# Transposing the attention weights by DMA instead of by TensorE, from the tenth group on

## The chip, the cores and the metric

The kernel runs on one core of a Trainium2 chip. A core has a matrix engine (TensorE, PE in the profile; its weight loads are shown apart as PEld), a vector engine (VectorE, DVE), a scalar engine (ScalarE, ACT), GpSimd (POOL) and SyncE (SP), each with its own instruction queue that is worked off in order, and 16 DMA engines that all queues of transfers share. The engines meet only at semaphores. The metric is the device time of one execution in microseconds. Before the change it was 306.21 us (median of three runs, 305.25 to 306.86).

## The reference

Two parts run one after the other. The first is attention within chunks of 64 tokens: q, k and v are 8 batches x 8 heads x 576 tokens x 64, and each chunk attends only to itself. The second is a two-layer network on the 4608 tokens of 512 channels that the first part gives.

```python
scores = scale * np.matmul(q_c, k_c.transpose(0, 1, 2, 4, 3))
scores = scores - np.max(scores, axis=-1, keepdims=True)
attn = np.exp(scores)
attn = attn / (np.sum(attn, axis=-1, keepdims=True) + 1e-09)
out = np.matmul(attn, v_c)
...
h = x @ w_in            # 4608x512 @ 512x2048
g = np.maximum(0.01 * h, h)
return (g @ w_out).astype(np.float32)   # @ 2048x512
```

## The kernel before

The tokens are cut into 36 groups of 128 (G, L54): two chunks for all eight heads. The network takes them in blocks of 128, 256 and 512 tokens (BLOCKS, L57). Everything is kept in SBUF as fp16; the sums are fp32 in PSUM.

**A group's attention** is a chain of stages, each a function with one letter:

- Loads and layout: groups 0 to 8 are loaded by L80 and transposed by TensorE (stage_t, L235); from group 9 on (UD, L53) whole batches are loaded by L98 from POOL's queue in pieces of 32 channels, and VectorE's block transposes bring them in place (stage_dq L273, stage_dk L281). v is loaded by L111.
- stage_s (L286): eight matmuls give the scores, tile Sp (L291).
- stage_m (L296): VectorE takes the maximum (mx, L299) and subtracts it (sh, L301).
- stage_x (L305): ScalarE takes the exponential (ex, L307).
- stage_n (L309): VectorE sums (z, L312), inverts (L314, L316) and multiplies: en (L318), the normalised weights, 128 queries x (8 heads and chunks x 64 keys), fp16.
- stage_e (L322): TensorE transposes en in four 128x128 pieces into a PSUM tile, tpe (L326).
- stage_c (L329): VectorE copies tpe to SBUF as et (L332).
- stage_v (L335): eight matmuls with the block-diagonal v tile VB as weights and et as the moving side give xp (L341), the attention's output, transposed.
- stage_a (L352): ScalarE copies xp into xT (L354), the network's input, and raises the count of tokens that the network may use.

tpe and xp share one PSUM buffer (tag "ox").

**The network** is cut into chunks of work, which `fill(n)` (L211) takes from a list in order, as far as the tokens are there. A first-layer chunk (mm1, L161) makes a 128x512 tile hT (L171) and ScalarE's leaky ReLU of it, gT (L178). A second-layer chunk (mm2, L182) is four of the sixteen matmuls into oP (L187); after the fourth, ScalarE copies oP to osb (L196) and SP issues the store to memory (L198). One chunk of the large blocks holds four matmuls with a moving side of 512 columns.

**The order** is written out by hand: there is no scheduler, so the order of the calls is the order on each engine. Groups 0 to 5 are in a list of letters (FRONT, L395). From then on one turn of the loop at L408 holds three groups at three stages, with network chunks between them:

```python
stage_s(it - 1); stage_m(it - 1)     # scores, maximum of one group
fill(2); stage_x(it - 1)
stage_e(it - 2); stage_c(it - 2)     # transpose of the group before
...                                  # layout of group it on VectorE
stage_n(it - 1)                      # en of the group of the scores
fill(2)
stage_v(it - 2); stage_a(it - 2)
fill(3 if dve else 2)
```

So en of a group is made late in one turn, is transposed in the first half of the next turn and used by stage_v in the middle of that turn. After the loop, L436 works off what is left of the network. SP's queue carries the first load of q (L138) and the 36 stores of osb, nothing else.

Of the kernel before, what the change touches and what calls it, by code (L numbers as in the profile page):

```python
# [8 lines left out]
FP16 = mybir.dt.float16  # L9
# [7 lines left out]
def kernel(  # L17
# [21 lines left out]
    nc = tc.nc  # L39
# [5 lines left out]
    CH = 64  # L45
# [5 lines left out]
    NVB = 2  # L51
    NIN = 9
    UD = 9  # L53
    G = 2 * CH  # L54

    NU = n_tok // G
    BLOCKS = [128] * 8 + [256] * 4 + [512] * 5  # L57

    sbp = ctx.enter_context(tc.tile_pool(name="k_sb", bufs=1))
# [11 lines left out]
    def load_qk(u):  # L71

        both = []
        for name, src in (("q_in", q), ("k_in", k)):
            t = sbp.tile([128, H, D], FP16, name=name, tag=name, bufs=NIN)
            r0, r1 = u * G, (u + 1) * G
            cut = min(-(-r0 // S) * S, r1) if r0 % S else r1
# [58 lines left out]
    for eng, name, src in ((nc.sync, "q_f", q), (nc.scalar, "k_f", k)):  # L136
        t = sbp.tile([128, H, D], FP32, name=name)
        eng.dma_start(out=t, in_=src[0, :, 0:G, :].rearrange("h p d -> p h d"))  # L138
        first.append(t)
# [21 lines left out]
    def mm1(j, a):  # L161
        tb, r0 = BLOCKS[j], START[j]
        nf = 512 // tb
        if j not in gT:
            tag, bufs, pad = ("gS", 6, 128) if tb == 128 else ("gT", 2, 512)
            gT[j] = sbp.tile([128, NFC, tb], FP16, name="gT", tag=tag, bufs=bufs, padded_shape=[128, NFC, pad])
        hT = psp.tile([128, nf, tb], FP32, name="hT", tag="mm", bufs=4)
        for i in range(nf):
            fc = nf * a + i
            for t in range(NT):  # L170
                nc.tensor.matmul(  # L171
                    out=hT[:, i, :],
                    lhsT=w_inT[:, t, fc * 128:(fc + 1) * 128],
                    rhs=xT[:, t, r0:r0 + tb],
                    start=(t == 0),
                    stop=(t == NT - 1),
                )
        nc.scalar.activation(  # L178
            out=gT[j][:, nf * a:nf * a + nf, :], in_=hT, func=AFT.Prelu, bias=0.0, scale=1.0, alpha=0.01
        )  # L180

    def mm2(j, ti, part):  # L182
        if part == 0:
            oP[j, ti] = psp.tile([128, d_model], FP32, name="oP", tag="mm", bufs=4)
        o = oP[j, ti]
        for fc in range(part * 4, part * 4 + 4):
            nc.tensor.matmul(  # L187
                out=o,
                lhsT=gT[j][:, fc, ti * 128:(ti + 1) * 128],
                rhs=w_outT[:, fc, :],  # L190
                start=(fc == 0),
                stop=(fc == NFC - 1),
            )
        if part == NFC // 4 - 1:
            osb = sbp.tile([128, d_model], FP32, name="osb", tag="osb", bufs=3)
            nc.scalar.activation(out=osb, in_=o, func=AFT.Copy, bias=0.0, scale=1.0)  # L196
            r0 = START[j] + ti * 128
            nc.sync.dma_start(out=out[r0:r0 + 128, :], in_=osb)  # L198
# [12 lines left out]
    def fill(n):  # L211
        for _ in range(n):
            if not chunks:
                return
            kind, j, a, p = chunks[0]
            if START[j] + BLOCKS[j] > state["tokens"]:
                return
            chunks.pop(0)
            if kind == "mm1":
                mm1(j, a)  # L220
            else:
                mm2(j, a, p)
# [12 lines left out]
    def stage_t(u):  # L235
        qt, kt = qk.pop(u)
        qp = psp.tile([128, 4, 2, CH], FP16, name="qp", tag="qp", bufs=1)
        kp = psp.tile([128, 4, 2, CH], FP16, name="kp", tag="kp", bufs=1)
        for i in range(4):
            nc.tensor.transpose(out=qp[:, i, :, :], in_=qt[:, 2 * i:2 * i + 2, :], identity=ident)  # L240
        for i in range(4):
            nc.tensor.transpose(out=kp[:, i, :, :], in_=kt[:, 2 * i:2 * i + 2, :], identity=ident)  # L242
        QP[u], KP[u] = qp, kp
# [21 lines left out]
    def cuts(u):  # L265
        r0, r1 = u * G, (u + 1) * G
        cut = min(-(-r0 // S) * S, r1) if r0 % S else r1
        return [(a // S, a % S, (a - r0) // CH, (z - a) // CH) for a, z in ((r0, cut), (cut, r1)) if a < z]

    def stage_dq(u, s):  # L270
        qz = QZ[u % NQZ]
        for b, at, e0, n in cuts(u):
            nc.vector.transpose(  # L273
                out=qz[s * CH:(s + 1) * CH, :, e0:e0 + n, s, :],
                in_=qkd[b][0][s * CH:(s + 1) * CH, :, at:at + n * CH].rearrange("p h (e t) -> p h e t", e=n),
            )

    def stage_dk(u):
        KT[u] = sbp.tile([128, 4, 2, CH], FP16, name="KT", tag="KT", bufs=3)
        for b, at, e0, n in cuts(u):  # L280
            nc.vector.transpose(  # L281
                out=KT[u][:, :, e0:e0 + n, :],
                in_=qkd[b][1][:, :, at:at + n * CH].rearrange("p h (e t) -> p h e t", e=n),
            )

    def stage_s(u):  # L286
        qz, kt = QZ[u % NQZ], KT.pop(u)
        Sp = psp.tile([128, 8, CH], FP32, name="Sp", tag="Sp", bufs=1)
        for i in range(8):
            g, e, m = i // 4, i // 2 % 2, i % 2  # L290
            nc.tensor.matmul(  # L291
                out=Sp[:, i, :], lhsT=qz[:, 2 * m + g, e, :, :], rhs=kt[:, 2 * m + g, e, :], start=True, stop=True
            )
        SP[u] = Sp

    def stage_m(u):  # L296
        Sp = SP.pop(u)
        mx = sbp.tile([128, 8], FP32, name="mx", tag="mx", bufs=2)
        nc.vector.tensor_reduce(out=mx, in_=Sp, axis=AXL.X, op=ALU.max)  # L299
        SH[u] = sbp.tile([128, 8, CH], FP32, name="sh", tag="sh", bufs=2)  # L300
        nc.vector.tensor_tensor(  # L301
            out=SH[u], in0=Sp, in1=mx.unsqueeze(2).to_broadcast((128, 8, CH)), op=ALU.subtract
        )

    def stage_x(u):  # L305
        E[u] = sbp.tile([128, 8, CH], FP16, name="ex", tag="ex", bufs=2)
        nc.scalar.activation(out=E[u], in_=SH.pop(u), func=AFT.Exp, bias=0.0, scale=SCL)  # L307

    def stage_n(u):  # L309
        ex = E.pop(u)  # L310
        z = sbp.tile([128, 8], FP32, name="z", tag="z", bufs=2)
        nc.vector.tensor_reduce(out=z, in_=ex, axis=AXL.X, op=ALU.add)  # L312
        ze = sbp.tile([128, 8], FP32, name="ze", tag="ze", bufs=2)
        nc.vector.tensor_scalar_add(out=ze, in0=z, scalar1=1e-9)  # L314
        zi = sbp.tile([128, 8], FP32, name="zi", tag="zi", bufs=2)
        nc.vector.reciprocal(out=zi, in_=ze)  # L316
        E[u] = sbp.tile([128, 8, CH], FP16, name="en", tag="en", bufs=2)
        nc.vector.tensor_tensor(  # L318
            out=E[u], in0=ex, in1=zi.unsqueeze(2).to_broadcast((128, 8, CH)), op=ALU.mult
        )  # L320

    def stage_e(u):  # L322
        en = E.pop(u)
        tpe = psp.tile([128, 4, 128], FP16, name="tpe", tag="ox", bufs=1)
        for i in range(4):
            nc.tensor.transpose(out=tpe[:, i, :], in_=en[:, 2 * i:2 * i + 2, :], identity=ident)  # L326
        TP[u] = tpe

    def stage_c(u):  # L329
        tpe = TP.pop(u)  # L330
        et = sbp.tile([128, 2, 2, 2, CH], FP16, name="et", tag="et", bufs=2)
        nc.vector.tensor_copy(out=et, in_=tpe)  # L332
        ET[u] = et

    def stage_v(u):  # L335
        et = ET.pop(u)
        xp = psp.tile([128, NT, 2, CH], FP32, name="xp", tag="ox", bufs=1)
        for e in range(2):
            b, c = divmod(2 * u + e, NCH)
            for t in range(NT):  # L340
                nc.tensor.matmul(  # L341
                    out=xp[:, t, e, :],
                    lhsT=VB[b % NVB][:, t, c, :],
                    rhs=et[:, t // 2, e, t % 2, :] if u < UD else et[:, t % 2, e, t // 2, :],
                    start=True,
# [6 lines left out]
    def stage_a(u):  # L352
        xp = XP.pop(u)
        nc.scalar.activation(out=xT[:, :, u * G:(u + 1) * G], in_=xp, func=AFT.Copy, bias=0.0, scale=1.0)  # L354
        state["tokens"] = (u + 1) * G

# [51 lines left out]
    for it in range(6, NU + 2):  # L408
        dve = UD <= it < NU
        if it <= NU:  # L410
            stage_s(it - 1)
            stage_m(it - 1)
        if dve:
            stage_dq(it, 0)
        fill(2)
        if it <= NU:
            stage_x(it - 1)
        stage_e(it - 2)
        stage_c(it - 2)
        if dve:  # L420
            stage_dq(it, 1)
            stage_dk(it)
        elif it < UD:
            stage_t(it)
            stage_q(it)
            stage_k(it)
        if it <= NU:
            stage_n(it - 1)
        fill(2)
        stage_v(it - 2)  # L430
        stage_a(it - 2)
        fill(3 if dve else 2)
        for b in range(3, B):
            if it == 9 * b // 2 - 4:
                load_qk_batch(b)
# [31 lines left out]
```

## Time and profile before

| | |
|---|---|
| Median of the runs | 306.21 us |
| The profiled execution | 305.16 us, of which 303.4 us is the span from first to last instruction |
| PE matmul, busy | 291.9 us, 2616 instructions |
| VectorE, busy | 194.5 us, 368 instructions |
| ScalarE, busy | 155.6 us, 267 instructions |
| Granted TensorE clock | 0.999 |
| DMA moved | 28.45 MB, 177500 packets |
| tpe matmuls (L326) | 144, 219 ns each |
| et copies (L332) | 36, 417 ns each |

The duration of a matmul in this table is from its start to the modelled end of its result. Matmuls overlap one another, so what one costs in TensorE's queue is the distance from its start to the next one's start, not this duration. The page's list of groups gives busy time, mean duration, and the idle time of the engine just before the group with what ended it; the timeline gives starts and lengths in order; the list of DMA issues gives the time from issue to landing.

### The profile page before, as it was taken

How to read it: one execution, taken by the hardware profiler on the slowest of the kernel's cores; microseconds unless marked ns; L12 is line 12 of the kernel's file. 1: busy time of each engine (PE TensorE's matmuls, PEld its weight loads, DVE VectorE, ACT ScalarE, POOL GpSimd, SP SyncE). 2: the span in 40 equal slices, each digit the busy share in tenths (PEclk: the TensorE clock that was granted, in tenths of full speed). 3: DMA queues.
4: the chain of work that ended last, by engine and by line, in shares of the span. 5: the costliest groups of instructions: out<-in, count | busy, mean ns of one | idle time of the engine just before them, and what ended most of it. 6: DMA issues, size and time to landing. Idle time of an engine off the chain costs nothing.

```text
span 303.4 us, 6278 instructions
## 1 busy us (share of the span) xinstructions
PE 291.9 (96%) x2616; PEld 181.8 (60%) x2616; DVE 194.5 (64%) x368; ACT 155.6 (51%) x267; POOL 119.6 (39%) x148
## 2 busy tenths in 40 slices
PE   5879999999999999999999999999999999999994
PEld 5878965777777676868555555555555554444441
DVE  3766876778888888788888887888888840000000
ACT  5346753555556473636377337723773377226411
POOL 8557656999008832970088329700000000000000
PEclk9999999999999999999999999999999999999999
DMA  9999999999909992999099939991101110011011
GB/s 129 167 192 166 197 161 177 166 139 159 131 37 59 127 120 41 127 110 100 35 91 95 115 82 123 80 97 69 37 0 37 69 37 0 35 70 36 0 69 70
DMA packets 177500, 28.45 MB, mean 94 GB/s; under 512 B 168768, under 2 KB 172864, under 8 KB 177472
## 3 DMA queue, kind: packets, MB, share of 16 engines
q0 software_dynamic: 170208, 18.10, 105.9%
q1 hardware_dynamic: 6224, 9.70, 9.0%
q8 instruction: 20, 0.33, 0.4%
q10 hardware_dynamic: 1040, 0.26, 0.4%
q14 instruction: 8, 0.07, 0.1%
HBM read 36.70 MB, written 9.44 MB: 152 GB/s over the span
## 4 chain that ended last, share of the span: by engine, by line
PE 83%; DMA 10%; POOL 4%; issue 1%; ACT 0%; ACTq 0%; POOLq 0%
PE oP L187 39%; PE hT L171 37%; DMA w_inT<-in_moe_w_in_dram 6%; DMA VB<-in_v_dram 5%; PE xp L341 2%; PE Sp L291 2%; PE tpe L326 2%; POOL VB L111 1%; POOL k_in L80 1%; POOL q_in L80 1%; POOL w_outT L130 1%; POOL w_inT L118 0%; ACT osb L196 0%; PE kp L242 0%; PE qp L240 0%
## 5 line engine op out<-in xcount | busy, mean ns | idle before, releaser
L171 PE MATMUL hT<-xT,w_inT 128*128 128x128 f16 (+2 forms) x1088 | 135.7, 279 | 1.8 <-DMA w_inT<-in_moe_w_in_dram 1.8
L187 PE MATMUL oP<-w_outT,gT 128*128 128x512 f16 x576 | 133.8, 379 | 0.1
L171 PEld LDWEIGHTS <-w_inT 128*128 128x128 f16 x1088 | 83.3, 98 | 37.4 <-issue 1.9
L178 ACT ACTIVATE gT<-hT 128x512 f16<-128x512 f32 x144 | 85.7, 597 | 37.5 <-PE hT L171 37.2
L187 PEld LDWEIGHTS <-gT 128*128 128x128 f16 x576 | 53.3, 98 | 55.3 <-issue 0.2
L98 POOL DMA_DIRECT2D q_d<-in_q_dram x48 | 38.8, 821 | 57.1 <-DVE QZ L273 53.3
L196 ACT ACTIVATE osb<-oP 128x512 f32<-128x512 f32 x36 | 21.5, 597 | 72.8 <-PE oP L187 69.9
L299 DVE TENSOR_REDUCE mx<-Sp 128x8 f32<-128x512 f32 x36 | 24.9, 691 | 33.2 <-PE Sp L291 33.1
L98 POOL DMA_DIRECT2D k_d<-in_k_dram x48 | 38.6, 815 | 0.4
L273 DVE STREAM_TRANSPOSE QZ<-q_d 64x512 f16<-64x512 f16 (+1 forms) x60 | 38.2, 644 | 0.8
L354 ACT ACTIVATE xT<-xp 128x512 f16<-128x512 f32 x36 | 21.4, 594 | 18.7 <-PE xp L341 18.7
L307 ACT ACTIVATE ex<-sh 128x512 f16<-128x512 f32 x36 | 22.5, 625 | 9.4 <-DVE sh L301 9.2
L312 DVE TENSOR_REDUCE z<-ex 128x8 f32<-128x512 f16 x36 | 23.5, 653 | 3.5 <-ACT ex L307 3.4
L318 DVE TENSOR_TENSOR en<-ex,zi 128x512 f16<-128x512 f16 x36 | 24.9, 692 | 1.2
L301 DVE TENSOR_TENSOR sh<-Sp,mx 128x512 f32<-128x512 f32 x36 | 24.9, 691 | 1.2
L111 POOL DMA_DIRECT2D VB<-in_v_dram x16 | 18.5, 1164 | 6.1 <-PE xp L341 6.1
L281 DVE STREAM_TRANSPOSE KT<-k_d 128x512 f16<-128x512 f16 (+1 forms) x30 | 19.4, 654 | 0.8
L332 DVE COPY et<-tpe 128x512 f16<-128x512 f16 x36 | 15.0, 417 | 5.6 <-PE tpe L326 5.5
L341 PEld LDWEIGHTS <-VB 128*128 128x128 f16 x288 | 13.2, 98 | 7.3 <-issue 0.7
L291 PEld LDWEIGHTS <-QZ 128*128 128x128 f16 x288 | 12.9, 98 | 5.3
L361 PE MATMUL idle<-ident 128*128 128x128 f16 x160 | 12.0, 240 | 3.8 <-POOL ident masks.py:199 3.8
L341 PE MATMUL xp<-et,VB 128*128 128x64 f16 x288 | 14.4, 193 | 0.5 <-DVE et L332 0.3
(32 smaller groups left out, 128.0 us busy)
## 6 DMA issues: line engine op xcount, KB each, us to landing
out_dram<-osb SPq DMA_DIRECT2D x36, 256.0 KB, 2.0
VB<-in_v_dram POOLq DMA_DIRECT2D x16, 288.0 KB, 6.2
q_d<-in_q_dram POOLq DMA_DIRECT2D x48, 72.0 KB, 4.0
k_d<-in_k_dram POOLq DMA_DIRECT2D x48, 72.0 KB, 3.9
w_inT<-in_moe_w_in_dram POOLq DMA_DIRECT2D x8, 256.0 KB, 9.5
w_outT<-in_moe_w_out_dram POOLq DMA_DIRECT2D x4, 512.0 KB, 9.0
q_in<-in_q_dram POOLq DMA_DIRECT2D x7, 128.0 KB, 10.6
k_in<-in_k_dram POOLq DMA_DIRECT2D x7, 128.0 KB, 10.0
```

The source lines that it names most:

```text
L98: nc.gpsimd.dma_start(out=t[p0:p0 + 32, m, :, :, :].rearrange("p h b d -> p (h b) d"), in_=src[b, h0:h0 + 2, :, dh * 32:dh * 32 + 32].rear ...
L111: nc.gpsimd.dma_start(out=VB[b % NVB][m * CH:(m + 1) * CH, :, :, m * CH:(m + 1) * CH].rearrange("p h c d -> p (h c) d"), in_=v[b, m * H // ...
L171: nc.tensor.matmul(out=hT[:, i, :], lhsT=w_inT[:, t, fc * 128:(fc + 1) * 128], rhs=xT[:, t, r0:r0 + tb], start=(t == 0), stop=(t == NT - 1),)
L178: nc.scalar.activation(out=gT[j][:, nf * a:nf * a + nf, :], in_=hT, func=AFT.Prelu, bias=0.0, scale=1.0, alpha=0.01)
L187: nc.tensor.matmul(out=o, lhsT=gT[j][:, fc, ti * 128:(ti + 1) * 128], rhs=w_outT[:, fc, :], start=(fc == 0), stop=(fc == NFC - 1),)
L273: nc.vector.transpose(out=qz[s * CH:(s + 1) * CH, :, e0:e0 + n, s, :], in_=qkd[b][0][s * CH:(s + 1) * CH, :, at:at + n * CH].rearrange("p ...
L299: nc.vector.tensor_reduce(out=mx, in_=Sp, axis=AXL.X, op=ALU.max)
L301: nc.vector.tensor_tensor(out=SH[u], in0=Sp, in1=mx.unsqueeze(2).to_broadcast((128, 8, CH)), op=ALU.subtract)
L307: nc.scalar.activation(out=E[u], in_=SH.pop(u), func=AFT.Exp, bias=0.0, scale=SCL)
L312: nc.vector.tensor_reduce(out=z, in_=ex, axis=AXL.X, op=ALU.add)
L318: nc.vector.tensor_tensor(out=E[u], in0=ex, in1=zi.unsqueeze(2).to_broadcast((128, 8, CH)), op=ALU.mult)
L341: nc.tensor.matmul(out=xp[:, t, e, :], lhsT=VB[b % NVB][:, t, c, :], rhs=et[:, t // 2, e, t % 2, :] if u < UD else et[:, t % 2, e, t // 2, :],
```

## The change

From group 9 on (a new constant UE) stage_e and stage_c are not called. In their place stage_et is called at the end of the turn before, right behind stage_n: one DMA on SP's queue reads en from SBUF, 128 x 512 fp16, and writes it transposed into et. et is laid out so that stage_v, which does not change, finds the pieces where it did. et has three buffers instead of two, and the small gT tiles (tag "gS", of the blocks of 128 tokens) five instead of six.

```diff
     UD = 9
+    UE = 9
...
-            tag, bufs, pad = ("gS", 6, 128) if tb == 128 else ("gT", 2, 512)
+            tag, bufs, pad = ("gS", 5, 128) if tb == 128 else ("gT", 2, 512)
...
     def stage_c(u):
         tpe = TP.pop(u)
-        et = sbp.tile([128, 2, 2, 2, CH], FP16, name="et", tag="et", bufs=2)
+        et = sbp.tile([128, 2, 2, 2, CH], FP16, name="et", tag="et", bufs=3)
         nc.vector.tensor_copy(out=et, in_=tpe)
         ET[u] = et
+
+    def stage_et(u):
+        en = E.pop(u)
+        et = sbp.tile([128, 2, 2, 2, CH], FP16, name="et", tag="et", bufs=3)
+        nc.sync.dma_start_transpose(
+            out=et.rearrange("p g e s j -> p (g e) (s j)"), in_=en.rearrange("p i j -> p (i j)")
+        )
+        ET[u] = et
...
-        stage_e(it - 2)
-        stage_c(it - 2)
+        if it - 2 < UE:
+            stage_e(it - 2)
+            stage_c(it - 2)
...
             stage_n(it - 1)
+            if it - 1 >= UE:
+                stage_et(it - 1)
         fill(2)
         stage_v(it - 2)
```

## The prediction, made before the changed kernel had run

> **What bounds the kernel now.** I read the page's first two parts, then the chain, then the waits of PE, then the timeline of one turn.
>
> ```profile
> PE 291.9 (96%) x2616; PEld 181.8 (60%) x2616; DVE 194.5 (64%) x368; ACT 155.6 (51%) x267; POOL 119.6 (39%) x148
> ...
> PEclk9999999999999999999999999999999999999999
> DMA  9999999999909992999099939991101110011011
> ...
> PE 83%; DMA 10%; POOL 4%; issue 1%; ACT 0%; ACTq 0%; POOLq 0%
> PE oP L187 39%; PE hT L171 37%; DMA w_inT<-in_moe_w_in_dram 6%; DMA VB<-in_v_dram 5%; PE xp L341 2%; PE Sp L291 2%; PE tpe L326 2%; POOL VB L111 1%; POOL k_in L80 1%; POOL q_in L80 1%; POOL w_outT L130 1%; POOL w_inT L118 0%; ACT osb L196 0%; PE kp L242 0%; PE qp L240 0%
> ```
>
> The chain is on PE for 83% of the span; its DMA and POOL pieces all lie ahead of 46.2 us, where the loads end. The clock is full throughout. PE's list of waits holds seven entries of 7.1 us in all, every one before 46 us. So from turn 10 to the end PE never waits, and its queue is the time: what is taken from it is gained, and what it is made to wait for is lost. The price of a stage on PE is the distance between starts in one turn:
>
> ```profile
> 142.42 0.40 PE L291 MATMUL Sp<-KT,QZ 128*128 128x64 f16 x8
> 142.65 1.89 PE L187 MATMUL oP<-w_outT,gT 128*128 128x512 f16 x8
> 144.38 0.39 PE L326 MATMUL tpe<-ident,en 128*128 128x128 f16 x4
> 144.60 1.89 PE L187 MATMUL oP<-w_outT,gT 128*128 128x512 f16 x8
> 146.33 0.40 PE L341 MATMUL xp<-et,VB 128*128 128x64 f16 x8
> 146.56 2.75 PE L187 MATMUL oP<-w_outT,gT 128*128 128x512 f16 x12
> 149.15 0.40 PE L291 MATMUL Sp<-KT,QZ 128*128 128x64 f16 x8
> ...
> 151.11 0.39 PE L326 MATMUL tpe<-ident,en 128*128 128x128 f16 x4
> ...
> 153.06 0.40 PE L341 MATMUL xp<-et,VB 128*128 128x64 f16 x8
> ```
>
> A turn is 6.73 us (142.42 to 149.15). The four transposes take 0.22 of it (144.38 to 144.60), not the 0.39 printed, which runs to the last result. On VectorE in the same turn:
>
> ```profile
> 144.81 0.42 DVE L332 COPY et<-tpe 128x512 f16<-128x512 f16 x1
> 145.26 0.71 DVE L273 STREAM_TRANSPOSE QZ<-q_d 64x512 f16<-64x512 f16 x1
> ...
> 147.75 0.69 DVE L318 TENSOR_TENSOR en<-ex,zi 128x512 f16<-128x512 f16 x1
> ```
>
> en of the group scored at 142.42 is done at 148.44; its xp starts at 153.06. These 4.62 us are the room into which the DMA must fit. Over groups 9 to 35 the room is 3.94 (group 27) to 4.74 us, mostly 4.5 to 4.6.
>
> **What goes.** The instruction lists of both kernels show 27 times four weight loads and four matmuls missing on PE and nothing moved. That is 27 x 0.22 = 5.9 us of the queue (2616 matmuls become 2508). By the chain, which gives tpe 2.3% of 303.4 us for 36 groups, 0.19 each, it would be 5.2; the distance is direct, so I take 5.9. It cannot be over 27 x 0.39 = 10.5. The 27 copies (417 ns, 11.3 us of DVE) gain nothing themselves: no PE row waits for DVE here. But en comes 0.45 earlier in its turn (the copy's start to the next start). The room becomes: turn 6.51, plus Sp to xp 3.91 - 0.22 = 3.69, less Sp to en's end 6.02 - 0.45 = 5.57; **4.63 us**, as before.
>
> **What comes.** Each group gets one DMA on SP's queue behind en, and xp waits for it. PE is in order, so behind xp stand the rest of the turn's network chunks and the next scores. Call T the time from en's end until xp may start. If T is over the room, PE stalls. From Sp to its en is 5.57, then T, then from xp to the Sp two turns after the first 2.82 (146.33 to 149.15): two turns take 8.39 + T. A turn is the larger of 6.51 and (8.39 + T)/2. The stall begins at T = 4.63; at T = 5.07 a turn is as long as today's and the gain is gone; each further us costs 0.5 us a group, 13.5 us in all.
>
> The trace has no transposing DMA, so T is bounded from DMA rows:
>
> ```profile
> out_dram<-osb SPq DMA_DIRECT2D x36, 256.0 KB, 2.0
> VB<-in_v_dram POOLq DMA_DIRECT2D x16, 288.0 KB, 6.2
> q_d<-in_q_dram POOLq DMA_DIRECT2D x48, 72.0 KB, 4.0
> ...
> q_f<-in_q_dram SPq DMA_DIRECT2D x1, 256.0 KB, 3.8
> ```
>
> Low end: the store of osb, same queue, twice the bytes in rows of 2 KB, 2.0 us. The new DMA reads 128 KB; its runs on both sides are 128 fp16, 256 B, so 512 pieces. The row with pieces of that size is q_f (64 fp32): 1024 of them on SP's queue land after 3.8 us. Half of the difference gives T = 2.0 + 1.8/2 = 2.9. High end: if the transposing cut its writes to single elements, 65,536 pieces. q_d (1152 pieces of 64 B, at best 2.9 us) and VB (2304 of 128 B, at best 5.0) differ by 1.8 ns a piece, which makes some 119 us, a turn of 64 and over 1,500 us more in all. I take 2.9, the nearest row in queue and piece size; 1.7 us of room stay over.
>
> The Trainium skill's DMA: Bandwidth & Descriptors (Latency and other measured facts; Anatomy of one DMA) gives transposing DMAs 261 GB/s and a DMA some 2 us of fixed cost; by that T is an estimated 2.5, hidden too.
>
> **What stands beside it.** Loads of q, k and v run beside about half of the groups. Stores in the same phases show what an SP transfer suffers: 2.0 us without loads; 3.3 to 3.6 from 91 to 106 us and 2.6 to 3.1 from 119 to 133 us, beside q_d and k_d; 5.3 and 5.0 for two beside v. With 1.0 to 1.6 more, T is 3.9 to 4.5, still inside. With 3.0 to 3.3 more it is 5.9 to 6.2, and a single such group stalls PE by 1.3 to 1.6 us. The v loads (five from 74 to 202 us) each meet about one group, whose room is the smallest (4.0 in group 18, 3.94 in 27); some stores beside v show nothing (2.0 from 106 to 119 us). I put one us on all of it.
>
> SP's queue: the last store ahead of each DMA comes from the turn's first fill; its osb is done by about 2.7 us after Sp, en at 5.57, so the DMA is not held. Stores behind it wait up to 1.3 us for en (osb 147.13, en 148.44); osb has three buffers at one store per four chunks (3.45 us), so some 10 us pass before a buffer is needed. en has two buffers: VectorE would be held only from T = 13.0 - 0.7 = 12.3 up. The third et buffer and the gS tile less cost nothing: block 5's first layer, the first to reuse a gS tile, follows the second layer of blocks 0 to 4.
>
> **Sum.** 305.16 (the profiled execution; 303.4 span and 1.8 around it) - 5.9 + 1.0 = 300.3. The shown median, 306.21, lies 1.05 higher; from it the same sum gives 301.3. I predict the middle, **300.8 us**.
>
> **Rivals.**
> 1. *The DMA outlasts the room in every group: slower.* In place: xp behind et. It decides from T = 5.07. At the VB row's 6.2 a turn is 7.30 and the time 305.2 + 27 x 0.57 = 320. For: many short pieces make DMAs slow in these rows, and a transposing write may be cut finer than 256 B. Against: 128 KB is less than half of VB's bytes and a quarter of its pieces. Chance 0.16.
> 2. *The four 128x128 blocks go one after another*, each as a DMA of its own, 2.0 us by the store: T = 8.0, a turn of 8.20, 305.2 + 27 x 1.47 = 345. For: four column blocks go to four places of et. Against: stores of 128 rows land together after 2.0. Anything slower still is counted here. Chance 0.12. Beside this stands the Trainium skill's VectorE: DVE Perf Modes (The three transpose paths; Rules for kernel authors): it prices a DMA transpose of one 128x128 block at 1309 ns against 390 on TensorE and prefers TensorE where PSUM will do. As an estimate, four in a row are 5.24 us, a turn of 6.82 and 307.5: this rule speaks against the change. No row here shows it.
> 3. *The loads eat the gain.* If all 13 groups beside loads suffer what the two stores beside v did, T = 6.2 there and each turn gives 0.79 back: 305.2 - 5.9 + 10.2 = 309.5. If half of them do, 304.4. Chance 0.12, a half of it within 0.5% of before.
>
> **How the numbers follow.** My forecast has 0.60. A measurement of this kernel can tell about 0.5% (1.5 us) from no change. Faster by more: 0.60 and a little of rival 3, 0.63. Within: the rest of that half and the mildest of rivals 1 and 2 around T = 5.1, 0.09. Slower: 0.28. The range: its low end is the sum with no stall and a run's scatter of 0.8, 298.5 (the bound by 10.5 is unlikely, since the next matmul starts 0.22 later); its high end is at 313, which takes in rival 3 and rival 1 up to T = 5.6, and leaves out rival 2 and most of rival 1.
>
> **What the profile after would show.** Right: 2508 PE matmuls, 341 DVE instructions, DVE 183 us busy; no row of tpe after group 8; SP with 27 more issues landing after 2 to 4 us; a turn of 6.5 us; PE without waits for et, or 1 to 2 us of them beside the v loads. Wrong: a line "PE xp <- DMA et" of many us, turns of over 6.73, and PE digits of 8 or less between slices 10 and 33; then T, read from issue to landing, says which rival it is. Wrong another way: late stores (ACT's osb waiting for a buffer) or VectorE waiting at en. The forecast fails if the landing time is above 5 us; nothing else on PE's path changes.

## The result, and the profile after

The changed kernel takes 309.52 us (median of four runs, 307.0 to 311.33) where the kernel before takes 305.81; the ratio is 1.0101, with a 95% interval of 1.0065 to 1.0137. It is slower by about 1%. The forecast was 300.8.

The page of the changed kernel (its lines are numbered one to twelve higher than before; L350 is now stage_v's matmul), parts 1, 2, 4 and 5; in part 5 the last field is PE's idle time just before the group and what ended it:

```profile
span 307.4 us, 6115 instructions
...
PE 286.9 (93%) x2508; PEld 175.0 (57%) x2508; DVE 184.1 (60%) x341; ACT 154.8 (50%) x267; POOL 119.5 (39%) x148
...
PE   5869999999999979998999989899999999999994
...
PE 70%; DMA 23%; POOL 4%; issue 1%; ACT 0%; ACTq 0%; POOLq 0%
...
L350 PE MATMUL xp<-et,VB 128*128 128x64 f16 x288 | 14.4, 193 | 8.0 <-DMA et<-en 7.3
```

The work went as foretold: 2508 matmuls, 341 VectorE instructions. But PE's row of digits, all 9 before from slice 4 to the last but one, now has a 7 and 8s between slices 15 and 26, and DMA has 23% of the chain instead of 10. The chain in order of time says which DMA, and when; these are its pieces on et (start, length):

```profile
95.30 4.89 DMA et<-en
...
109.50 6.22 DMA et<-en
...
131.12 4.79 DMA et<-en
...
137.55 6.61 DMA et<-en
...
159.50 4.62 DMA et<-en
...
172.71 6.09 DMA et<-en
...
194.44 5.20 DMA et<-en
```

Seven of the 27 transposing DMAs are on the path, all issued before 200 us; the last reload of v is issued at 200.39. In what follows, turn n is the one that begins with the scores of group n. Behind the last reload the timeline of PE shows turns as forecast:

```profile
209.01 0.40 PE L292 MATMUL Sp<-KT,QZ 128*128 128x64 f16 x8
209.24 3.62 PE L188 MATMUL oP<-w_outT,gT 128*128 128x512 f16 x16
212.70 0.40 PE L350 MATMUL xp<-et,VB 128*128 128x64 f16 x8
212.93 2.75 PE L188 MATMUL oP<-w_outT,gT 128*128 128x512 f16 x12
215.52 0.40 PE L292 MATMUL Sp<-KT,QZ 128*128 128x64 f16 x8
```

This turn is 6.51 us. Turn 15, while a v reload is in flight; GpSimd issues it as soon as the xp that needed the old v is done (first row), and the transposing DMA on the path follows at 109.50:

```profile
107.34 2.31 POOL L112 DMA_DIRECT2D VB<-in_v_dram  x2 [1.81 <-PE xp L350]
...
109.62 0.40 PE L292 MATMUL Sp<-KT,QZ 128*128 128x64 f16 x8
109.85 2.78 PE L172 MATMUL hT<-xT,w_inT 128*128 128x256 f16 x24
112.47 1.03 PE L188 MATMUL oP<-w_outT,gT 128*128 128x512 f16 x4
115.76 0.39 PE L350 MATMUL xp<-et,VB 128*128 128x64 f16 x8 [2.27 <-DMA et<-en]
115.99 2.75 PE L188 MATMUL oP<-w_outT,gT 128*128 128x512 f16 x12
118.58 0.40 PE L292 MATMUL Sp<-KT,QZ 128*128 128x64 f16 x8
```

This one is 8.96. (The room was smaller here than usual, too: en of group 14 ended 6.37 us after its scores instead of 5.66.) From the scores of group 9 to those of group 35 the kernel before takes 175.66 us (67.76 to 243.42), this one 178.74 (69.33 to 248.07), and this one without loads (e3 below) 170.07. So 5.6 us were gained there and 8.7 lost again in stalls, each the turn's length less the same turn's in e3: 2.42 (turn 15), 1.67 (turn 19) and 1.68 (turn 24) behind v reloads, 1.18, 0.60, 0.47 and 0.40 behind loads of q and k, and little else.

### The profile page after: what moved, and what is told of

Read it like the earlier page. It is cut to its first block, busy times and chain, and to the rows that moved or that the text cites. A ratio compares the mean times of both kernels' runs of the same rounds, so it can differ in the third digit from the quotient of the medians.

```text
span 307.4 us, 6115 instructions
## 1 busy us (share of the span) xinstructions
PE 286.9 (93%) x2508; PEld 175.0 (57%) x2508; DVE 184.1 (60%) x341; ACT 154.8 (50%) x267; POOL 119.5 (39%) x148
## 4 chain that ended last, share of the span: by engine, by line
PE 70%; DMA 23%; POOL 4%; issue 1%; ACT 0%; ACTq 0%; POOLq 0%
PE oP L188 35%; PE hT L172 31%; DMA et<-en 13%; DMA w_inT<-in_moe_w_in_dram 6%; DMA VB<-in_v_dram 5%; PE xp L350 3%; PE Sp L292 2%; POOL VB L112 1%; POOL k_in L81 1%; POOL q_in L81 1%; POOL w_outT L131 1%; PE tpe L327 0%; ACT osb L197 0%; POOL w_inT L119 0%; PE kp L243 0%
## 5 line engine op out<-in xcount | busy, mean ns | idle before, releaser
L172 PE MATMUL hT<-xT,w_inT 128*128 128x128 f16 (+2 forms) x1088 | 133.5, 279 | 2.7 <-DMA w_inT<-in_moe_w_in_dram 2.6
L188 PE MATMUL oP<-w_outT,gT 128*128 128x512 f16 x576 | 132.2, 379 | 0.3 <-DMA w_outT<-in_moe_w_out_dram 0.3
L350 PEld LDWEIGHTS <-VB 128*128 128x128 f16 x288 | 13.0, 98 | 16.2 <-issue 7.9
L350 PE MATMUL xp<-et,VB 128*128 128x64 f16 x288 | 14.4, 193 | 8.0 <-DMA et<-en 7.3
L292 PE MATMUL Sp<-KT,QZ 128*128 128x64 f16 x288 | 14.3, 193 | 0.0
```

Source lines behind the costliest of these rows:

```text
L172: nc.tensor.matmul(out=hT[:, i, :], lhsT=w_inT[:, t, fc * 128:(fc + 1) * 128], rhs=xT[:, t, r0:r0 + tb], start=(t == 0), stop=(t == NT - 1),)
L188: nc.tensor.matmul(out=o, lhsT=gT[j][:, fc, ti * 128:(ti + 1) * 128], rhs=w_outT[:, fc, :], start=(fc == 0), stop=(fc == NFC - 1),)
L292: nc.tensor.matmul(out=Sp[:, i, :], lhsT=qz[:, 2 * m + g, e, :, :], rhs=kt[:, 2 * m + g, e, :], start=True, stop=True)
L350: nc.tensor.matmul(out=xp[:, t, e, :], lhsT=VB[b % NVB][:, t, c, :], rhs=et[:, t // 2, e, t % 2, :] if u < UD else et[:, t % 2, e, t // 2, :],
```

## The experiments

**Theory M**: the whole loss is PE waiting at xp for et, where the transposing DMA meets loads. **Rival S**: the stores on the same queue hold that DMA. **Rival D**: the DMA disturbs other work. **Rival G**: the changed buffer counts cost the time.

### Without the loads: e1, e2, e3 and the control e4

```diff
-            if c == NCH - 1 and b + NVB < B:      # e1, e3, e4
-                load_v(b + NVB)
...
-                load_qk_batch(b)                  # e2, e3, e4
+                qkd[b] = qkd[2]
```

> The changed kernel without the reloads of v: stage_v issues none, so the batches from the third on multiply with v of the first two, and 12 of the 16 v DMAs are left out. Theory M (the whole loss is the wait of xp for et, where the transposing DMA meets loads, above all v): the three long stalls beside v (2.45, 1.74 and 1.68 us, turns of 8.96, 8.25 and 8.19 us) go, so some 5.9 us, to 303 to 304 us, ratio to before about 0.993; the waits beside q and k stay (1.2, 0.6, 0.5, 0.4 us). Rival S (the transposing DMA is held by the stores that share SP's queue): no change, 309. Rival D (the transposing DMA itself disturbs other work): no change, or under 1 us.

> The changed kernel without the loads of q and k for batches 3 to 7: VectorE transposes batch 2 again in their place. Theory M: only the stalls beside q_d and k_d go (1.18, 0.61, 0.48 and 0.40 us, 2.7 in all); those beside v stay; 306 to 307 us, ratio about 1.002. Rival S and rival D: no change, 309.

> The changed kernel without either (v from the third batch on, q and k from batch 3 on). Theory M: every transposing DMA after the first loads lands in about 2.4 us as those after 208 us did, no stall, turns of 6.51 us: 299.5 to 300.5 us, ratio about 0.981. Rival S: stalls stay where stores are near, over 305. Rival D: over 303.

> The control: the kernel before without the same loads (v from the third batch on, q and k from batch 3 on). Nothing on TensorE waits for these loads there, so all theories expect the time of before, ratio 0.998 to 1.002. If it is faster by over 1 us, the loads cost before something too, and e3 must be compared with this run.

| | us | ratio to before |
|---|---|---|
| e1, no v reloads | 303.47 | 0.9911 (0.9871 to 0.9950) |
| e2, no q and k | 310.50 | 1.0159 (1.0121 to 1.0197) |
| e3, neither | 299.68 | 0.9798 (0.9765 to 0.9831) |
| e4, the kernel before, neither | 306.57 | 1.0015 (0.9993 to 1.0037) |

The issue line of stage_et, L339, in the trace of the changed kernel and then in that of e3, time from issue to landing:

```profile
DMA to landing us min/median/max: 2.4/4.1/6.6
```

```profile
DMA to landing us min/median/max: 2.4/2.4/4.0
```

Turn 15 of e3:

```profile
107.43 0.40 PE L292 MATMUL Sp<-KT,QZ 128*128 128x64 f16 x8
...
110.28 1.03 PE L188 MATMUL oP<-w_outT,gT 128*128 128x512 f16 x4
111.14 0.40 PE L350 MATMUL xp<-et,VB 128*128 128x64 f16 x8
111.38 2.75 PE L188 MATMUL oP<-w_outT,gT 128*128 128x512 f16 x12
113.97 0.40 PE L292 MATMUL Sp<-KT,QZ 128*128 128x64 f16 x8
```

e3 settles the main question. With the same DMAs, the same stores and no loads beside them, 25 of the 27 DMAs land within 2.4 to 2.5 us, no turn stalls (turn 15 is 6.54), and the change brings about the 2% that was forecast. e4 shows that the loads cost the kernel before nothing. Rival D expected over 303 in e3 and is out; rival S expected over 305 and is out too.

The two other DMAs of e3, of groups 11 and 13, land after 4.0 us, still inside the room. A packet of 16 KB of the instruction queue runs beside each of them; this is the stretch of the first, 86.9 to 90.9 us:

```profile
q8 instruction: 1, 0.02, 1.5%
...
et<-en SPq DMA_TRANSPOSE x1, 4.0
```

Group 11 of the changed kernel has the same packet and no load beside it, and lands after 4.2 us. That the packet is the cause is not tested.

e1 came out as expected in time (303.47 for 303 to 304). Its stalls, all beside q and k, add up to 3.7 us where 2.7 were expected: one DMA there (group 26) landed after 6.0 us and cost 1.8, with no v in flight. So it is not v alone that makes a landing long.

e2 missed. M expected 306 to 307, since only stalls beside q and k would go. They did go, but the stalls beside v grew: now all five v reloads stall a turn (by 2.75, 3.93, 1.67, 1.40 and 1.80 us, 11.6 in all) where three of five did. (In the two new ones the DMA was issued 2.2 and 1.3 us behind the reload's start; in the changed kernel it was within 0.2 us of it.) So the two shares don't add up: q and k alone cost 303.47 - 299.68 = 3.8 us, v alone 10.8, both 9.8. Part of it is a second effect, seen on PE in e2 (timeline, then stretches of 1 us; the third number from the end is the granted clock):

```profile
114.81 1.03 PE L188 MATMUL oP<-w_outT,gT 128*128 128x512 f16 x4
117.92 0.39 PE L350 MATMUL xp<-et,VB 128*128 128x64 f16 x8 [2.08 <-DMA et<-en]
118.15 4.44 PE L188 MATMUL oP<-w_outT,gT 128*128 128x512 f16 x12
122.43 0.40 PE L292 MATMUL Sp<-KT,QZ 128*128 128x64 f16 x8
```

```profile
118.00:119.00 1.00, 1.00 (x12) 0.55 (x12) 0.00 (x0) 0.60 (x1) 0.00 (x0) 0.99 0.09 19
119.00:120.00 1.00, 1.00 (x4) 0.40 (x3) 0.00 (x0) 0.00 (x0) 0.00 (x0) 0.50 0.57 113
```

Twelve matmuls that take 2.6 us elsewhere take 4.28 (118.15 to 122.43): about a us after the wait the clock fell to 0.50 and stayed there for 3.4 us. By the starts, the 3.93 of this turn are 2.2 of waiting and 1.7 of slow matmuls.

### Buffers, stores, and a plain copy: e5, e6, e8, e9

> The kernel before with the change's buffer counts alone (three et, five gS), transposes still on TensorE. Theory M and the prediction: no effect, ratio 0.998 to 1.002. Rival G (the smaller gS or other addresses made the first 60 us later, 1.6 us in the profiled pair): ratio about 1.005.

```diff
-            tag, bufs, pad = ("gS", 6, 128) if tb == 128 else ("gT", 2, 512)
+            tag, bufs, pad = ("gS", 5, 128) if tb == 128 else ("gT", 2, 512)
...
-        et = sbp.tile([128, 2, 2, 2, CH], FP16, name="et", tag="et", bufs=2)
+        et = sbp.tile([128, 2, 2, 2, CH], FP16, name="et", tag="et", bufs=3)
```

e5 takes 306.22 us, 1.0016 (0.9994 to 1.0038): rival G is out. That group 9's scores came 1.6 us later in the profiled pair is not the change: over the profiles of all these kernels they lie between 67.2 and 69.5 us, 69.04 in e12 below, which is the kernel before up to there but for the buffers.

> The changed kernel with the 36 stores issued from ScalarE's queue instead of SP's, so that the transposing DMAs have SP's queue for themselves. Theory M: the loads are what delays them, so landing beside v stays at about 6 us; 308 to 311 us, ratio about 1.01. Rival S: landing falls to 2.4 to 4 us everywhere, stalls go, about 300 us.

```diff
-            nc.sync.dma_start(out=out[r0:r0 + 128, :], in_=osb)
+            nc.scalar.dma_start(out=out[r0:r0 + 128, :], in_=osb)
```

e6 takes 311.96 us, 1.0210 (1.0175 to 1.0245). With SP's queue to itself the transposing DMA still lands after 5.3 to 6.7 us beside four of the five v reloads, and after 7.3 once beside k_d. Rival S is out again. This was even slower than the change and just above the 308 to 311 that M expected; why is not shown.

> The changed kernel with a plain DMA from en to et, same queue, same bytes, nothing transposed (so the weights are multiplied untransposed): 128 rows of 1 KB instead of 512 pieces of 256 B. If what delays the DMA beside loads is its number of pieces, this one lands in 2.0 to 3 us there and the stalls go: about 300 us. If any DMA on that queue is delayed alike beside loads, landing beside v stays at 5 to 6 us and the time at 306 to 310.

> As the plain copy (nothing transposed), but cut into 512 pieces of 256 B, the size in which the transposing DMA reads: et's rows are padded so that the four pieces of a row can't be joined. If the number of pieces is what makes the transposing DMA land after 6.1 to 6.6 us beside v (the plain copy: at most 4.8), this one lands there after about 6 and the time is 307 to 310. If it is the transposing, this one stays near the plain copy: at most 5 us, 301 to 302.5.

```diff
-        nc.sync.dma_start_transpose(
-            out=et.rearrange("p g e s j -> p (g e) (s j)"), in_=en.rearrange("p i j -> p (i j)")
-        )
+        nc.sync.dma_start(                                           # e8
+            out=et.rearrange("p g e s j -> p (g e s j)"), in_=en.rearrange("p i j -> p (i j)")
+        )
...
+        et = sbp.tile([128, 4, 144], FP16, name="et", tag="et", bufs=3)[:, :, 0:128]   # e9
+        nc.sync.dma_start(out=et, in_=en.rearrange("p (i s) j -> p i (s j)", s=2))
```

The issue rows of the three kernels (the issue's own time in ns min/median/max) with the time to landing: the changed kernel, e8, e9.

```profile
L339 SPq DMA_TRANSPOSE et<-en x27: 1189/1192/1601, 75.5 to 253.3; - x27
...
DMA to landing us min/median/max: 2.4/4.1/6.6
```

```profile
L339 SPq DMA_DIRECT2D et<-en x27: 464/471/527, 75.1 to 245.6; - x27
...
DMA to landing us min/median/max: 1.9/3.2/4.8
```

```profile
L339 SPq DMA_DIRECT2D et<-en x27: 593/600/686, 74.6 to 247.4; - x27
...
DMA to landing us min/median/max: 2.3/3.1/5.9
```

| | alone | issued 0.9 to 2.2 us after a v reload | time | ratio |
|---|---|---|---|---|
| e8, plain, 128 pieces | 1.9 | 4.0, 4.2, 4.5, 4.8 | 301.33 | 0.9872 (0.9834 to 0.9910) |
| e9, plain, 512 pieces | 2.3 | 4.3, 4.5, 5.9 | 303.02 | 0.9902 (0.9866 to 0.9937) |
| the change, transposing | 2.4 | 6.1, 6.2, 6.6 | 309.52 | 1.0101 (1.0065 to 1.0137) |

e8 came between its two forecasts, nearer the first: it landed after up to 4.8 us beside loads and took 301.33 us. e9 lies a little above its lower forecast (at most 5 us, 301 to 302.5) and far below the other. Alone, the number of pieces explains the landing time (2.3 against 2.4). Beside loads it explains a little at most (e8 and e9 overlap in their intervals); most of the difference, some 6.5 us, belongs to the transposing form of the DMA. Whether that is the crossing in the DMA path or the issue, which holds SP 0.6 us longer, these runs don't tell apart.

### More room: e7, its control e10, and e11

> The changed kernel with stage_v and stage_a moved behind the turn's last three network chunks (from group 9 on). The room between en and xp grows by 3 x 0.865 = 2.6 us to 7.1 us; the longest wait seen was 6.73. Theory M: no stall left, turns of 6.51 us, 299 to 301 us, ratio about 0.981. Rival D: the DMA's disturbance stays, 303 or more. If v's reloads come so much later that they meet the DMA longer, stalls of up to 1 us beside v stay.

> The control for e7: the kernel before, transposes on TensorE, with the same move of stage_v and stage_a behind the turn's last network chunks. Theory M: no wait to hide there, so 305.3 to 306.5, ratio 0.998 to 1.002; all of e7's gain is then the transposes taken off TensorE. If the move alone gains, this is below 304.

> The changed kernel with stage_v behind one of the turn's last chunks instead of three: room 4.54 + 0.865 = 5.4 us. Theory M, with the waits of the changed kernel's profile: groups 14, 18 and 23 (6.34, 6.73, 6.20 from en to xp) still stall by 0.9, 1.3 and 0.8, 3.1 us; the waits beside q and k (up to 5.3) are gone: 299.7 + 3 = 302 to 304, ratio about 0.99. If the loss were not the wait, it would stay near 309.

```diff
         fill(2)
+        if it - 2 >= UE:                 # UD in e10; fill(1) in e11
+            fill(3 if dve else 2)
         stage_v(it - 2)
         stage_a(it - 2)
-        fill(3 if dve else 2)
+        if it - 2 < UE:                  # e11: no condition, one chunk less
+            fill(3 if dve else 2)
```

| | room, us | us | ratio to before |
|---|---|---|---|
| the change | 4.54 | 309.52 | 1.0101 (1.0065 to 1.0137) |
| e11, one chunk later | 5.40 | 301.37 | 0.9855 (0.9807 to 0.9903) |
| e7, three chunks later | 7.13 | 300.29 | 0.9817 (0.9782 to 0.9852) |
| e10, the kernel before, three chunks later | | 306.40 | 1.0016 (0.9991 to 1.0042) |

PE's longest waits in e7, us in total, times, longest:

```profile
PE idle L370 <- POOL ident masks.py:199: 3.8, 1, 3.8
PE hT L172 <- DMA w_inT<-in_moe_w_in_dram: 1.8, 1, 1.8
PE tpe L327 <- DVE en L319: 0.6, 1, 0.6
```

No wait for a DMA of et is left (the longest landing is 6.0 us), and from the scores of group 9 to those of group 35 the kernel takes 170.07 us, as without loads. e7 keeps every load and store and every transposing DMA and is **1.8% faster than the kernel before** (1.5 to 2.2%) and 3% faster than the change; e10 shows that the move alone gains nothing. This is the mend: not a faster DMA, but 2.6 us more work between its issue and its reader.

e11 did better than expected (301.37, not 302 to 304). The move also shifts when v reloads start, since they are issued behind stage_v: in e11 the DMA was issued from 0.5 us before to 0.5 after them, and landed after 2.5 to 5.3 us instead of 6.1 to 6.6 in the three long stalls of the change. In e7 it goes 1.2 to 1.4 us ahead of four of the five and lands after 2.4 to 3.1.

### The DMA only where no loads are: e12

> The changed kernel with the DMA from group 28 on only, behind the last loads (UE = 28). Theory M: no stall, 8 x 0.22 = 1.8 us gained: 303.7 to 304.5, ratio about 0.994. Rival D: no gain.

```diff
-    UE = 9
+    UE = 28
```

e12 takes 303.56 us, 0.9916 (0.9889 to 0.9943): a gain of 1.7 to 3.4 us, the expected 1.8 at its edge. The turns go from 6.73 to 6.51 where the DMA begins, and all eight land after 2.4 to 2.5 us.

### Moving only v's start: e13

> The changed kernel with its order and room kept, but each reload of v now starts behind the transposing DMA of the following group: GpSimd first reads one column of that group's et. In the traces so far a transposing DMA issued 0.9 to 2.2 us after the start of a v reload landed after 5.7 to 6.7 us, one issued 1.2 us before it after 2.4 to 3.1, one issued over 5 us after it after 2.4 to 3.3. Theory M with the phase as cause: the reload starts some 2.5 us behind the DMA's issue and 4 us ahead of the next one, which should land after 3 to 4.4; the three long stalls go, those beside q and k stay: as without the v reloads, 302.5 to 304.5, ratio about 0.99. Rival (v delays the DMA wherever it lies): the stalls move to the next group, each 1 to 1.5 us: 306 to 309.

```diff
             if c == NCH - 1 and b + NVB < B:
+                if u + 1 in ET:
+                    nc.gpsimd.tensor_copy(out=scrap, in_=ET[u + 1][:, 0, 0, 0, 0:1])
                 load_v(b + NVB)
```

e13 takes 311.51 us, 1.0182 (1.0135 to 1.0228), outside both ranges. The three long stalls went, as the theory of the phase had it: the DMA in front of each reload landed after 3.2 to 4.0 us. The next one, where it came 3.3 us behind the reload's start, took 5.7 and 4.1, and only the first of these made a stall, of 1.7 us; so the rival's move of the stalls to the next group shows once in five. The other 12 of 13.8 us lie beside q and k (1.6 of them are matmuls at the halved clock), where two DMAs took 6.9 and 7.5 us (5.2 at most in the changed kernel).

Not all of that need come from the moved reloads. The first of them starts at 80.8 us, and in this profile the loads were slower before that: q_d issued between 60 and 70 us landed after 7.3 us in the median (6.3 in the changed kernel), and the DMA of group 9 after 6.1 (4.4). So e13 shows that moving the reload was no mend; it does not settle whether the phase is a cause. What makes one overlap cost 4 us and another 7 stays open.

## Why the prediction was wrong, step by step

- **PE is the time; four transposes cost 0.22 us a group: right.** Turns of 6.51 us, as forecast; e3 against before is 6.1 us for a forecast 5.9.
- **The room: right.** 4.63 us forecast, 4.54 measured (xp 212.70 less en's end 208.16). The stalls begin just above it, as the formula says.
- **T from the nearest rows: nearly right.** 2.9 forecast, 2.4 measured alone. The four blocks did not run one after another (rival 2), and not every group outlasted the room (rival 1). The Trainium skill's VectorE: DVE Perf Modes (The three transpose paths) prices one 128x128 block at 1309 ns; here a DMA of four blocks lands in 2.4 us, so this figure can't be added up by blocks. That page's preference for TensorE (Rules for kernel authors) came out right as the change stands, and wrong in e7, which is 1.8% faster than the kernel before.
- **"What stands beside it" is the step that failed: "I put one us on all of it".** Measured: 8.7. The mechanism was in the text, with the rows for it, and so was the sign of failure, a landing above 5 us; the size was wrong, for four reasons.
  - I carried over what a *store* suffers (1.0 to 1.6 us more beside q and k, 3.0 to 3.3 beside v). The transposing DMA suffers more: 1.7 to 2.8 more beside q and k (4.1 to 5.2 us), and 3.7 to 4.2 in the three that stalled beside v (6.1 to 6.6).
  - With a room of 4.5 this difference is the whole matter: a landing of 4.5 is free and one of 6.2 costs 1.7 us.
  - The meeting with v is built in. The reload is issued right behind xp, and in the three of five turns that stalled en of the next group ended 1.5 to 2.7 us after that xp had started.
  - The text itself said that each v load meets about one group. By its bound, five groups at 1.3 to 1.6 would have been 7 us. I set that aside because "some stores beside v show nothing (2.0 from 106 to 119 us)", and this was misread. In the trace of the kernel before, one store is issued in that stretch, at 116.1, and the two v DMAs issued at 106.3 and 107.4 had landed by 113.6. The store ran alone. The rows of those v DMAs, then of the store:

```profile
L111 POOL DMA_DIRECT2D VB<-in_v_dram x2: 1150/1156/1162, 106.3 to 107.4; - x2
...
DMA to landing us min/median/max: 5.0/5.6/6.2
```

```profile
L198 SPq DMA_DIRECT2D out_dram<-osb x1: 332/332/332, 116.1 to 116.1; - x1
...
DMA to landing us min/median/max: 2.0/2.0/2.0
```

- **Rival 3 was the answer**, with a chance of 0.12. That its high figure, 309.5, is the result to the tenth is luck. It has 13 groups lose 0.8 us each, 10.2 in all; seven lost up to 2.4 each, 8.7 in all, and the profiled run also came to group 9 later by 1.6 us, which is scatter (e5).
- **SP's queue, the stores, the buffers: right that they cost nothing** (e3 for the queue and the stores, e5 for the buffers).
- **A cost that the prediction did not have:** the clock was halved right after a wait of a few us in e2, e6 and e13. The profiled run of the change shows none of it (clock 1.0). Of its other runs the one at 311.33 has a clock of 0.994, but those at 307.0 and 309.88 have 0.999 and 1.0: the clock does not explain the scatter of its runs, and what does is not shown.

## What to carry to other kernels

A DMA that replaces work on the limiting engine has to be priced at its worst landing time beside the kernel's other transfers, not alone, and for its own kind of transfer: what a store suffers beside the same loads was too small a price. Compare this worst time with the room between producer and reader; where it doesn't fit, put more of the limiting engine's work between them before giving the change up. And look at what is issued right behind the reader: a load released there met the next DMA in three of five turns, and in all five of e2.

## What the runs showed of the hardware

- A transposing DMA of 128 x 512 fp16 within SBUF holds SP for 1.19 us and lands after 2.4 us alone, hardly later than a plain copy in as many pieces (2.3). Beside loads it lands after up to 7.5 us (e13), the plain copy in as many pieces after 5.9 at most (e9) and in whole rows after 4.8 (e8). The Trainium skill's Advanced Engine Details and Errata (X-Bar Transpose) calls transposing DMAs as fast as regular ones: that agrees for the DMA alone, and does not beside loads, where the measurement decides.
- Every landing of the transposing DMA over 3 us that has no load beside it (3.2 to 4.4 us; groups 11 and 13 of e3, group 13 of e2 and others) has a 16 KB packet of the instruction queue beside it.
- TensorE's granted clock fell to 0.50 for 3.4 us after waits of 2.1 us in e2, 2.4 in e6 and 3.0 in e13, and stayed at 1.00 after waits of 2.3 us in the changed kernel and 2.6 in e2 (the idle times that the trace prints). So the length of the wait alone does not decide. The Trainium skill's TensorE: Matmul & The Clock Gate (Part 1) describes a free-running window of about 3.4 us, after an idle one of which the rate is halved; the half rate and its length agree, the waits seen here are shorter than that window.
